# A scheduler's rules in a decay-attention and max-MoE kernel: VectorE and GpSimd kept apart, a price for matmuls that waited, new seeds

## The chip, the cores and the metric

The kernel runs on one core of one Trainium2 chip. The metric is the device time of one execution in microseconds (us), the median of several runs. The engines are TensorE (PE in the rows; its weight loads are PEld), VectorE (DVE), ScalarE (ACT), GpSimd (POOL) and SyncE (SP), which issues the DMAs.

## What is computed

Decayed causal attention over 8 batches of 8 heads, 576 positions, 64 columns a head; then a feed-forward block whose hidden layer is the largest of three products, over all 4608 tokens.

```python
scores = scale * np.matmul(q, k.transpose(0, 1, 3, 2))
cum = np.cumsum(np.log(np.clip(f, 0.0001, 1.0)), axis=-1)
scores = np.where(causal, -1e9, scores + cum[..., :, None] - cum[..., None, :])
attn = softmax(scores)
x = np.matmul(attn, v)            # then heads side by side: (4608, 512)
h = np.maximum(np.maximum(x @ w1, x @ w2), x @ w3)      # 512 -> 768
out = h @ w_out                                          # 768 -> 512
```

## The kernel before

The work is cut into 64 heads and 8 batches. A head's scores are built in two units of queries (256 and 320 wide) in PSUM banks `s`: a first pass of matmuls (`pass_a`, L730), the causal mask (on TensorE for the first 16 heads, on VectorE at L767 and L772 for the others), the column maxima on VectorE (`most`, L793 to L798), a GpSimd all-reduce over the partitions (L808) and, behind the first batch, a GpSimd copy of the result into a row of the query operand (L811), then a second pass that subtracts the maximum (L730 again, or L757 in the first batch) and the exponential on ScalarE (L829). From head 16 the sums of the exponentials are added on VectorE (L838 to L845) and all-reduced on GpSimd (L853); a row of them goes through DMA into a small tile `sc`, where VectorE adds a constant and inverts it (L1021, L1022). `values_pair` multiplies with v (L899).

A batch's feed-forward block follows when its heads are done. `gemm1` (L1059) runs 12 matmuls into one of four banks (`mp0`, `mp1`, `mp2`, `t`) for each of the three weights; ScalarE copies the first bank into `tm` (L1068), VectorE takes the maximum of the other two with `tm` (L1070), and each of these steps gives its bank back. Then a high and a low part are split off (L1073 on ScalarE, L1075 on VectorE) for `gemm2` (L1090). Heads of later batches are prepared meanwhile: VectorE transposes q and k (L619) and splits them (L625).

At the start, 20 matmuls on an identity (`warm_up`, L520) are there as filling; the first eight heads come in raw and TensorE turns them, six matmuls for each half (`turn_head`, L540), into the same four banks, which VectorE and ScalarE copy out (L548, L550). `decay` clips f on VectorE (L491), takes the logarithm on ScalarE (L493), the running sum on VectorE (L496), and ScalarE writes two rows of it (L500). Constants are set by memsets on GpSimd (L447, L461 to L473) and VectorE (L476).

The order of all this is not written out. Each step is added to a `Plan` with its engine, a cost in ns, its operands and a priority. `emit` walks through the steps like a clockwork: at the earliest moment an engine is free, it gives it the ready step with the best rank, books its cost (scaled and padded by `ROOM`), and lets a model of TensorE's clock and a lag for each pair of engines decide when others become ready. The instructions are then issued in the order of the booked beginnings; on the chip each engine follows its own list, and semaphores do the waiting. `SEEDS` disturb the ranks a little, one random stream for each window of priorities; a zero leaves a window alone.

Of the kernel before, what the change touches and what calls it, by code (L numbers as in the profile page):

```python
# [11 lines left out]
F32 = mybir.dt.float32  # L12
# [4 lines left out]
ALU = mybir.AluOpType  # L17
# [38 lines left out]
class Plan:  # L56
# [10 lines left out]
    ROOM = {"PE": (1.0, 0), "ACT": (1.0, -20.0), "DVE": (1.0, 0.0), "POOL": (1.0, 400.0), "SP": (1.0, 0)}  # L67
# [4 lines left out]
    SEEDS = [9961, 6458, 701, 7690, 5056, 2474, 4633, 0, 366, 8932, 0, 0, 1279, 0, 0, 723, 0, 0, 419]  # L72
# [10 lines left out]
    def add(self, eng, cost, fn, r=(), w=(), prio=0.0, xfer=0.0, rows=128, short=0.0, light=False, take=(), drop=()):  # L83
# [16 lines left out]
        self.steps.append((eng, cost, fn, deps, prio, xfer, rows, short, light, take, drop))  # L100

    def emit(self):
# [27 lines left out]
        short = 0.0  # L130
        clock = GatedClock()
# [19 lines left out]
        while done < n:  # L151
# [27 lines left out]
            if self.steps[i][5]:  # L179

                t = max(t, lanes[-8])
            begin[i] = t
# [53 lines left out]
def kernel(  # L236
# [212 lines left out]
    def head_constants(i, prio):  # L449

        for key, ns, go in (
            (f"ks{i}", 380, lambda: nc.gpsimd.memset(KS(i)[:, :, S:SP].bitcast(F32), 0.0)),
            (f"qs{i}", 1100, lambda: nc.gpsimd.memset(QS(i)[96:P, :, :].bitcast(F32), 1.0)),
            (f"ks{i}", 1100, lambda: nc.gpsimd.memset(KS(i)[96:P, :, 0:S].bitcast(F32), 0.0)),
            (f"ks{i}", 660, lambda: nc.gpsimd.memset(KS(i)[96:97, 1, :].bitcast(F32), -1.0)),
        ):
            add("POOL", ns, go, w=[key], prio=prio)
# [12 lines left out]
    add("POOL", 1060, sums_constants, ["cs"], [f"rs{g}{u}" for g in range(2) for u in (1, 2)], 0.0)  # L470
    add("POOL", 1100, constants, w=["const"], prio=-9)
    add("POOL", 200, lambda: nc.gpsimd.memset(LESS.bitcast(F32), 0.0), w=["less"], prio=-9)
    add("POOL", 100, lambda: nc.gpsimd.memset(LESS[0:1].bitcast(F32), -1.0), w=["less"], prio=-9)  # L473
    for i in range(H):
        add("POOL", 525, lambda i=i: first_constants(i), w=[f"qf{i}/2"], prio=-9 + i)
        add("DVE", 605, lambda i=i: nc.vector.memset(KF[i][64:P, :], 0.0), w=[f"kf{i}/2"], prio=-5.5 + 0.1 * i)  # L476
    add("POOL", 1650, value_constants, w=[f"vn{i}" for i in range(4)], prio=-8)


    def decay():  # L480
# [11 lines left out]
            ["pf1"], ["pf1"], DP)  # L492
# [5 lines left out]
            ["pf1"], ["pf1"], DP)  # L498
        for n in range(2):
# [4 lines left out]
            ["pf1"], [f"u{KT - 1}"], DP)  # L504
        for n, e, dst in [(n, n + 1, KF[n][64:65, :]) for n in (2, 3)] + [
# [4 lines left out]
            ["pf1"], ["cs"], DP)  # L510
        add("DVE", 669, lambda: nc.vector.scalar_tensor_tensor(
            cs[:, 1, :], ft, -1.0, cs[:, 0, :].bitcast(F32), op0=ALU.mult, op1=ALU.subtract),
            ["pf1", "cs"], ["cs"], DP)
# [40 lines left out]
    def convert(x, low, top, kt, kl, kx, prio):  # L554
# [5 lines left out]
            y, low, 29, None, op0=ALU.logical_shift_right), [kt], [kl], prio)  # L560
        add("DVE", 1.1 * n + 75, lambda: nc.vector.scalar_tensor_tensor(
            x, top, 3, y, op0=ALU.logical_shift_left, op1=ALU.bitwise_or), [kt, kl], [kx], prio)

    def split(x, h, l, kx, kh, kl, gone, prio):
# [3 lines left out]
            l(), x.bitcast(F32), h().bitcast(F32), op=ALU.subtract), kx + [kh], [kl], prio)  # L568
# [41 lines left out]
    def load_quad(b, g, prio):  # L610
        for nm, src, sc in (("q", q, scale), ("k", k, 1.0)):
# [9 lines left out]
            if b < NB32:  # L621
# [5 lines left out]
                op0=ALU.mult, op1=ALU.subtract), [key + "0"], [key + "1"], prio)  # L627
# [73 lines left out]
    def scores(n, unit, prio):  # L701
# [101 lines left out]
        for a, w, bk, col, nb in d["first"]:  # L803
# [5 lines left out]
            gm, mt, P, bass.bass_isa.ReduceOp.max), [km, km + "a"], [kg], prio - CB)  # L809
        if not first:  # L810
            add("POOL", 130 + 0.9 * nq, lambda: nc.gpsimd.tensor_copy(  # L811
                QS(s)[96:97, 1, q0:q0 + nq], gm[96:97, :]), [kg], [kx], prio - CB)
# [34 lines left out]
        if unit == 2:  # L847
            add("ACT", act_cost(P), lambda: nc.scalar.activation(
                blocks_sum()[:, 0:P], px()[:, 0:P], AF.Copy), [pk], ["s2/0"], prio + SP_)
            add("DVE", dve_cost(P), add_blocks, [pk], ["s2/1"], prio + SP_)  # L850
        else:
            add("DVE", sum(dve_cost(w) + 125 for w in (320, 320, 192, 64)) - 125, add_blocks, [pk], ["s1"], prio + SP_)
        add("POOL", 520 + 5.1 * nq, lambda: nc.gpsimd.partition_all_reduce(  # L853
            Z[:, q0:q0 + nq], blocks_sum()[:, q0:q0 + nq], P, bass.bass_isa.ReduceOp.add), [f"s{unit}"], [f"z{unit}"], prio + SP_)
# [119 lines left out]
    def finish_rows(g, prio):  # L974
# [13 lines left out]
        for t in range(2):  # L988
# [3 lines left out]
            for j in range(2):  # L992
# [3 lines left out]
                U(pi)[:, q0:S], U(pi)[:, q0:S], r, op=ALU.mult), [key, ku], [ku], prio)  # L996

    def split_first(kt, unit, prio):
# [3 lines left out]
        else:  # L1002
# [3 lines left out]
            l(), U(kt)[:, cs], h().bitcast(F32), op=ALU.subtract), [ku, kh], [kl], prio)  # L1006
# [6 lines left out]
    def finish_pair(pi, prio):  # L1013
# [18 lines left out]
        add("DVE", dve_cost(S), lambda: nc.vector.tensor_tensor(U(i), U(i), R(), op=ALU.mult), [f"u{i}", "r"], [f"u{i}"], prio)  # L1032

    def split_x(b, prio):
        for kt in range(KT):
# [4 lines left out]
                xl(kt), U(i), xh(kt).bitcast(F32), op=ALU.subtract), [f"u{i}", f"xh{kt}"], [f"xl{kt}"], prio)  # L1040
# [6 lines left out]
    def gemm1(b, c0, cn, fb, parts, prio):  # L1047
# [24 lines left out]
        for hh, hl, kh, kl, a, d, w in parts:  # L1072
# [4 lines left out]
                [kt_, kh + str(fb)], [kl + str(fb)], prio)  # L1077
# [171 lines left out]
```

## Time and profile before

| what | us |
|---|---|
| median of 3 runs | 909.21 |
| lowest and highest | 906.84, 911.02 |
| the profiled execution | 907.82 |
| its span, first to last instruction | 906.0 |
| TensorE busy in the span | 886.8 (98%) |
| VectorE busy | 634.5 (70%) |
| GpSimd busy | 429.0 (47%) |
| ScalarE busy | 382.0 (42%) |

Busy time of TensorE is read with care: a matmul's end is modelled, and a matmul that follows closely on another overlaps it. So a wait of TensorE is read from the idle time in front of a matmul and from the distance of the starts after it.

### The profile page before, as it was taken

The page shows a single profiled execution, that of the slowest core. Times are in us where ns is not written, and L with a number is a line of the kernel's source. Part 1 is how long each engine was busy: PE and PEld are TensorE (multiplying, and loading weights), DVE is VectorE, ACT ScalarE, POOL GpSimd, SP SyncE. Part 2 cuts the span into 40 slices and gives each one's busy share as a digit, 9 for nine tenths or more (in the row PEclk, how much of TensorE's full clock was granted, in tenths as well). Part 3 has the DMA queues.
Part 4 walks back from the last instruction along what each step waited for, and adds up shares of the span by engine and source line. Part 5 has one row for each costly group of instructions (what it writes and reads, how often), then busy time and mean ns, then how long its engine had stood idle before and what let it go on. Part 6 is the DMA issues. An engine that isn't in the chain of part 4 may idle for free.

```text
span 906.0 us, 18239 instructions
## 1 busy us (share of the span) xinstructions
PE 886.8 (98%) x6614; PEld 806.4 (89%) x6614; DVE 634.5 (70%) x1386; ACT 382.0 (42%) x882; POOL 429.0 (47%) x380
## 2 busy tenths in 40 slices
PE   7999999999999999999999999999999999999998
PEld 5888988889988998899989898988989898998997
DVE  6899764577878786887878786777867867662211
ACT  4797543444433443444433443343334443441211
POOL 4564132327574657456564556455454555740000
PEclk8999999999999999999999999999999999999999
DMA  6965256455564355455454544544444554301010
GB/s 159 327 198 178 80 140 158 119 132 145 123 176 118 97 149 124 128 131 140 108 158 127 120 129 118 139 106 130 114 108 133 117 145 121 93 14 37 1 36 24
DMA packets 93371, 110.99 MB, mean 123 GB/s; under 512 B 52461, under 2 KB 56301, under 8 KB 93282
## 3 DMA queue, kind: packets, MB, share of 16 engines
q1 hardware_dynamic: 93282, 109.83, 46.1%
q8 instruction: 53, 0.87, 0.4%
q14 instruction: 36, 0.29, 0.1%
HBM read 50.22 MB, written 9.87 MB: 66 GB/s over the span
## 4 chain that ended last, share of the span: by engine, by line
PE 80%; DVE 13%; issue 2%; ACT 2%; DMA 2%; SPq 1%; POOL 1%; ACTq 0%; DVEq 0%
PE mp L1059 31%; PE mp L1090 12%; PE s L730 11%; PE t L1059 10%; PE mp L899 6%; PE t L1090 3%; PE t L899 3%; DVE hl L619 2%; DVE va_s L845 2%; DVE mx L798 2%; DVE tm L1070 1%; PE t L866 1%; DVE hl L625 1%; DMA vn<-in_v_dram 1%; DVE hml_r L1075 1%
## 5 line engine op out<-in xcount | busy, mean ns | idle before, releaser
L1059 PE MATMUL mp<-xh_r,w_r 128*128 128x320 f32 (+1 forms) x1624 | 379.9, 299 | 2.3 <-DVE tm L1070 1.9
L1059 PEld LDWEIGHTS mp<-xh_r,w_r 128*128 128x128 f32 x1624 | 278.0, 188 | 6.4 <-DVE tm L1070 3.1
L808 POOL PARTITION_ALL_REDUCE gm<-mx x131 | 158.0, 1207 | 234.8 <-DVE mx L798 98.4
L853 POOL PARTITION_ALL_REDUCE z<-va_s x96 | 194.9, 2031 | 128.0 <-DVE va_s L845 54.4
L1059 PE MATMUL mp<-xl_r,w_r 128*128 128x320 f32 (+1 forms) x812 | 240.2, 296 | 0.0
L1059 PEld LDWEIGHTS mp<-xl_r,w_r 128*128 128x128 f32 x812 | 152.9, 188 | 0.7
L1059 PE MATMUL t<-xh_r,w_r 128*128 128x320 f32 (+1 forms) x536 | 143.5, 299 | 1.0 <-DVE tm L1070 1.0
L730 PEld LDWEIGHTS s<-qs_r,ks_r 128*128 128x128 f32 (+1 forms) x784 | 115.7, 181 | 17.4 <-issue 9.3
L730 PE MATMUL s<-qs_r,ks_r 128*128 128x320 f32 (+4 forms) x784 | 128.3, 281 | 1.5 <-issue 0.8
L798 DVE TENSOR_TENSOR mx<-mx,s 128x320 f32<-128x320 f32 (+3 forms) x248 | 92.1, 371 | 21.5 <-ACT mx L805 7.7
L1059 PEld LDWEIGHTS t<-xh_r,w_r 128*128 128x128 f32 x536 | 97.8, 188 | 2.7 <-DVE tm L1070 2.3
L1090 PE MATMUL mp<-w_r,hmh_r 128*128 128x512 f32 (+1 forms) x324 | 100.0, 391 | 0.0
L1070 DVE TENSOR_TENSOR tm<-mp,tm 128x320 f32<-128x320 f32 (+1 forms) x143 | 64.6, 452 | 48.3 <-PE mp L1059 33.3
L1073 ACT ACTIVATE hmh_r<-tm 128x256 fp32r<-128x256 f32 x96 | 40.0, 417 | 101.9 <-DVE tm L1070 101.6
L1059 PE MATMUL t<-xl_r,w_r 128*128 128x320 f32 (+1 forms) x268 | 79.3, 296 | 0.0
L619 DVE STREAM_TRANSPOSE hl<-hl 128x576 f32<-128x576 f32 x56 | 67.8, 1244 | 3.5 <-DMA vn<-in_v_dram 3.1
L1068 ACT ACTIVATE tm<-mp 128x256 f32<-128x256 f32 (+1 forms) x76 | 31.0, 408 | 85.8 <-PE mp L1059 80.4
L1090 PEld LDWEIGHTS mp<-w_r,hmh_r 128*128 128x128 f32 x324 | 57.2, 188 | 10.1 <-issue 0.7
L1075 DVE TENSOR_TENSOR hml_r<-tm,hmh_r 128x256 fp32r<-128x256 f32 x96 | 48.6, 506 | 20.3 <-ACT hmh_r L1073 20.2
L1090 PE MATMUL mp<-w_r,hml_r 128*128 128x512 f32 (+1 forms) x162 | 62.5, 386 | 0.0
L829 ACT ACTIVATE pf<-s 128x512 f32<-128x512 f32 (+4 forms) x107 | 49.5, 506 | 27.8 <-PE s L730 24.2
L767 DVE TENSOR_TENSOR s<-s,mask 128x256 f32<-128x256 f32 x96 | 40.6, 424 | 27.8 <-PE s L730 27.4
(253 smaller groups left out, 1485.9 us busy)
## 6 DMA issues: line engine op xcount, KB each, us to landing
qs_r<-hl SPq DMA_DIRECT2D x168, 144.0 KB
ks_r<-hl SPq DMA_DIRECT2D x168, 144.0 KB
w<-in_moe_w_dram SPq DMA_DIRECT2D x9, 1024.0 KB
out_dram<-o_r SPq DMA_DIRECT2D x35, 256.0 KB
hl<-in_k_dram SPq DMA_DIRECT2D x14, 576.0 KB
hl<-in_q_dram SPq DMA_DIRECT2D x14, 576.0 KB
r_r<-rdram SPq DMA_DIRECT2D x56, 144.0 KB
vn<-in_v_dram SPq DMA_DIRECT2D x30, 128.0 KB
```

The source lines that it names most:

```text
L619: add("DVE", 1085, lambda e=e, tt=tt, xs=xs: nc.vector.transpose(tt[:, e], xs[:, e]), [key + "0"], [key + "1"], prio)
L730: nc.tensor.matmul(bank[bk][0:l.shape[-1], col:col + w], l, rhs(qa, w), start=start and bk not in begun, stop=stop, skip_group_check=True)
L767: nc.vector.tensor_tensor(x, x, mask.rearrange("p (o x) -> p o x", o=1).broadcast_to((P, 2, P)), op=ALU.add)
L798: nc.vector.tensor_tensor(mt[:, a:a + w], mt[:, a:a + w], bank[bk][:, col:col + w], op=ALU.max)
L808: add("POOL", 450 + 2.6 * nq, lambda: nc.gpsimd.partition_all_reduce(gm, mt, P, bass.bass_isa.ReduceOp.max), [km, km + "a"], [kg], prio - CB)
L829: add("ACT", act_cost(w), lambda bk=bk, w=w, col=col: nc.scalar.activation(px()[:, col:col + w], bank[bk][:, 0:w], AF.Exp, scale=sc), [kb[ ...
L853: add("POOL", 520 + 5.1 * nq, lambda: nc.gpsimd.partition_all_reduce(Z[:, q0:q0 + nq], blocks_sum()[:, q0:q0 + nq], P, bass.bass_isa.Reduc ...
L899: nc.tensor.matmul(t[D * j:D * j + D, qa:qa + w], vn[:, j, c, 0:D], prs[x][j][0]()[:, col:col + w], start=y == 0, stop=True, skip_group_ch ...
L1059: nc.tensor.matmul(m(), unit_w(i, fb)[:, w, kt, :], xx, start=kt == 0 and x == 0, stop=kt == KT - 1 and x == 2,)
L1070: add("DVE", dve_cost(cn), lambda m=m: nc.vector.tensor_tensor(t, m(), t, op=ALU.max), [km, kt_], [kt_], prio + EV, drop=(slot,))
L1075: add("DVE", dve_cost(w), lambda hh=hh, hl=hl, a=a, d=d, w=w: nc.vector.tensor_tensor(hl()[:, fb, d:d + w], t[:, a:a + w], hh()[:, fb, d:d ...
L1090: nc.tensor.matmul(BANKS[slot.bank][:, 0:cn], l[:, fb, cs], unit_o(fb)[:, r, ds], start=fb == 0 and x == 0, stop=fb == FT - 1 and x == 2,)
```

## The change

No instruction of the computation is added or taken away. What changes is the planner's bookkeeping, and with it the order.

- A step may carry a `port` time. Two-operand steps of VectorE, and the `tensor_scalar` steps that go from SBUF to SBUF, carry 1 ns, which stands for their whole length: while such a step is booked, no GpSimd step with a port begins. A GpSimd step carries the part in which it holds VectorE's marked steps off: all of a memset, `2.1 * nq - 30` ns of a maximum's all-reduce, `4.45 * nq - 180` of a sum's, `0.6 * nq + 70` of a copy.
- GpSimd's padding in `ROOM` goes from 400 ns a step to 130 ns.
- A matmul that begins over 20 ns after TensorE became free is booked with 105 ns more (`STALL`).
- The seeds are new; 16 of 19 windows are now disturbed, where it was 12.

```diff
-    ROOM = {"PE": (1.0, 0), "ACT": (1.0, -20.0), "DVE": (1.0, 0.0), "POOL": (1.0, 400.0), "SP": (1.0, 0)}
+    ROOM = {"PE": (1.0, 0), "ACT": (1.0, -20.0), "DVE": (1.0, 0.0), "POOL": (1.0, 130.0), "SP": (1.0, 0)}
...
+    STALL = 105.0
...
+            port = self.steps[i][11]
+            if port:
+
+                t = max(t, held[e])
             begin[i] = t
...
             end = t + cost
+            if port:
+                other = "POOL" if e == "DVE" else "DVE"
+                held[other] = max(held[other], t + port if e == "POOL" else end)
             if e == "PE":
-                end = clock.run(t, cost, self.steps[i][6])
+                end = clock.run(t, cost + (self.STALL if t > free[e] + 20 else 0.0), self.steps[i][6])
...
         add("POOL", 450 + 2.6 * nq, lambda: nc.gpsimd.partition_all_reduce(
-            gm, mt, P, bass.bass_isa.ReduceOp.max), [km, km + "a"], [kg], prio - CB)
+            gm, mt, P, bass.bass_isa.ReduceOp.max), [km, km + "a"], [kg], prio - CB, port=2.1 * nq - 30)
```

Ten lines are added to the file, so a line behind L491 stands ten lower in the code after: L520 is L530, L1070 is L1080. The orders were compared with buffer numbers and semaphores. `DVE_49` and the like name the engine (or DMA queue) whose semaphore is waited for.

The first place is TensorE at the start, from the last transposition of head 1 to those of head 3 (`w8` holds heads 0 and 1, `w9` heads 2 and 3). Before:

```order
L540 MATMUL mp2_120<-hdl_107,w8_103 64x96 x5
L520 LDWEIGHTS ident_63
L520 MATMUL s10_113<-ident_63 128x512
...
L540 MATMUL mp0_118<-hdl_107,w9_104 64x96 [waits DMAHW7_49,Activation_49]
L540 MATMUL mp0_118<-hdl_107,w9_104 64x96 x5
L540 MATMUL mp1_119<-hdl_107,w9_104 64x96 [waits DMAHW6_49,Activation_49]
```

Now:

```order
L550 MATMUL mp2_120<-hdl_107,w8_103 64x96 x5
L530 LDWEIGHTS ident_63
L530 MATMUL s10_113<-ident_63 128x512
...
L550 MATMUL mp0_118<-hdl_107,w9_104 64x96 [waits DMAHW7_49,DVE_49]
L550 MATMUL mp0_118<-hdl_107,w9_104 64x96 x5
L530 LDWEIGHTS ident_63
L530 MATMUL s10_113<-ident_63 128x512
...
L550 MATMUL mp1_119<-hdl_107,w9_104 64x96 [waits DMAHW6_49,Activation_49]
```

Before, seven fillers stand ahead of the transposition into `mp0`; now two stand ahead of it and five behind. The copies that empty `mp0` have changed places too: the transposition waited for ScalarE's copy as the second, and now for VectorE's.

The second place is VectorE and GpSimd at the start. VectorE before:

```order
L522 CAST hdl_107<-ident_63 128x128 [waits Pool_49]
L476 MEMSET ks1_68 64x576
L476 MEMSET xh_69 64x576 x2
L476 MEMSET xl_70 64x576
L491 TENSOR_SCALAR pf1_80<-pf1_80 65x576 [waits DMAHW1_49,DMAHW0_49]
...
L496 SCALAR_TENSOR_TENSOR pf1_80<-pf1_80 65x576 [waits Activation_49]
L548 COPY qs0_65<-mp0_118 64x288 [waits PE_49]
```

and now:

```order
L532 CAST hdl_107<-ident_63 128x128 [waits Pool_49]
L486 MEMSET ks1_68 64x576
L486 MEMSET xh_69 64x576 x2
L501 TENSOR_SCALAR pf1_80<-pf1_80 65x576 [waits DMAHW1_49,DMAHW0_49]
L486 MEMSET xl_70 64x576 x2
L506 SCALAR_TENSOR_TENSOR pf1_80<-pf1_80 65x576 [waits Activation_49]
L558 COPY qs0_65<-mp0_118 64x288 [waits Activation_49]
```

(between L491 and L496 before stood the second memset of `xl`). One memset moved from ahead of the clipping of f to behind it. GpSimd before:

```order
L447 MEMSET qs0_65 64x576 [waits Pool_49]
L472 MEMSET pl2_72 128x128 [waits Pool_49]
L461 MEMSET vn0_75 64x2x65 [waits Pool_49]
...
L473 MEMSET pl2_72 1x128
L447 MEMSET qs1_66 64x576 [waits Pool_49]
L447 MEMSET ks0_67 64x576
```

and now:

```order
L482 MEMSET pl2_72 128x128
L457 MEMSET qs0_65 64x576 [waits Pool_49]
L483 MEMSET pl2_72 1x128
L457 MEMSET qs1_66 64x576
L471 MEMSET vn0_75 64x2x65
...
L457 MEMSET ks0_67 64x576 [waits Pool_49]
```

The eight short memsets of the v buffers moved behind `qs1`, and four memsets in a row (`qs0` to `vn0`) now begin without a wait between them.

The third place is VectorE in the middle of the kernel, around the eleventh step of L1021. Before:

```order
L767 TENSOR_TENSOR s10_113<-s10_113,mask_64 128x2x128
L1021 TENSOR_SCALAR sc_94<-sc_94 64x18
L772 TENSOR_TENSOR s11_114<-s11_114,mask_64 128x64
L619 STREAM_TRANSPOSE hl_73<-hl_73 128x18x32
L1022 RECIPROCAL sc_94<-sc_94 64x18
L1070 TENSOR_TENSOR tm1_112<-mp2_120,tm1_112 128x320
```

and now:

```order
L777 TENSOR_TENSOR s2_116<-s2_116,mask_64 128x2x128
L1031 TENSOR_SCALAR sc_94<-sc_94 64x18
L803 COPY mx2_83<-s2_116 128x128
L805 TENSOR_REDUCE mx2_83<-s2_116 128x128
L1032 RECIPROCAL sc_94<-sc_94 64x18
L852 TENSOR_TENSOR va1_s_2091<-pf1_80 128x320
```

The next maximum that gives a bank back stood four steps behind L1021; now 16 steps lie between.

## Rows read from the trace of the kernel before

**Rows 1.** Busy time by stretch (PE, PEld, DVE, ACT, POOL; clock; DMA).

```profile
24.00:91.00 67.00, 62.95 (x512) 57.84 (x512) 61.24 (x104) 55.04 (x110) 35.79 (x32) 1.00 0.75 230
91.00:861.00 770.00, 763.64 (x5615) 694.86 (x5614) 551.22 (x1240) 308.13 (x731) 382.66 (x319) 1.00 0.46 117
```

**Rows 2.** TensorE's waits: us in total, times, longest; those for banks.

```profile
PE mp L1059 <- DVE tm L1070: 1.9, 4, 1.1
PE t L1059 <- DVE tm L1070: 1.0, 3, 0.7
...
PE mp L899 <- DVE tm L1070: 0.6, 1, 0.6
PE mp L899 <- ACT tm L1068: 0.6, 1, 0.6
...
PE t L899 <- DVE tm L1070: 0.4, 1, 0.4
PE mp L1059 <- ACT tm L1068: 0.3, 1, 0.3
```

**Rows 3.** Timeline, one wait of TensorE: start, us, engine, line; [idle before].

```profile
376.04 0.31 PE L1059 MATMUL mp<-xh_r,w_r 128*128 128x320 f32 x1
377.45 0.42 PE L1059 MATMUL mp<-xh_r,w_r 128*128 128x320 f32 x1 [1.10 <-DVE tm L1070]
377.70 0.31 PE L1059 MATMUL mp<-xl_r,w_r 128*128 128x320 f32 x1
377.85 0.45 PE L1059 MATMUL mp<-xh_r,w_r 128*128 128x320 f32 x2
```

**Rows 4.** Timeline of VectorE and GpSimd ahead of that wait.

```profile
374.34 1.37 DVE L1021 TENSOR_SCALAR sc<-sc 64x18 f32<-64x18 f32 x1
...
372.35 4.11 POOL L853 PARTITION_ALL_REDUCE z<-va_s  x2 [0.84 <-DMA sc<-z]
```

**Rows 5.** Shortest, median and longest of one line's steps on VectorE, ns.

```profile
L1021 DVE TENSOR_SCALAR sc<-sc x28: 139/160/1366, 133.6 to 813.3; 64x18 f32<-64x18 f32 x28
L1075 DVE TENSOR_TENSOR hml_r<-tm,hmh_r x96: 386/424/1502, 97.7 to 895.9; 128x256 fp32r<-128x256 f32 x96
L798 DVE TENSOR_TENSOR mx<-mx,s x248: 186/355/491, 20.0 to 799.3; 128x320 f32<-128x320 f32 x56, 128x192 f32<-128x192 f32 x56, 128x160 f32<-128x160 f32 x4, 128x32 f32<-128x32 f32 x4
```

**Rows 6.** Timeline of the start, VectorE.

```profile
2.82 0.23 DVE L522 CAST hdl<-ident 128x128 f32<-128x128 bf16 x1
...
5.04 0.54 DVE L476 MEMSET xl<- 64x576 f32 x1
5.61 3.21 DVE L491 TENSOR_SCALAR pf<-pf 65x576 f32<-65x576 f32 x1
...
10.85 0.43 DVE L548 COPY qs<-mp 64x288 f32<-64x288 f32 x1
```

**Rows 7.** Timeline of the start, GpSimd.

```profile
2.67 0.20 POOL L472 MEMSET pl<- 128x128 f32 x1
...
4.82 0.57 POOL L447 MEMSET qs<- 64x576 f32 x1
...
7.42 1.09 POOL L447 MEMSET xl<- 64x576 f32 x2
8.57 1.26 POOL L465 MEMSET ph<- 97x1152 f32 x1
```

**Rows 8.** Timeline of the start, ScalarE's first copy and TensorE.

```profile
11.07 0.41 ACT L550 ACTIVATE qs<-mp 64x288 f32<-64x288 f32 x1
...
13.34 1.83 PE L540 MATMUL mp<-hdl,w 96*64 96x96 f32 x24 [3.75 <-ACT qs L550]
```

**Rows 9.** Busy time by stretch around the clock's fall, columns as in the first.

```profile
10.34:13.76 3.42, 0.42 (x10) 0.42 (x12) 1.66 (x4) 3.33 (x8) 0.00 (x0) 1.00 0.33 76
13.76:20.58 6.82, 6.82 (x58) 6.51 (x55) 2.45 (x7) 3.28 (x9) 0.00 (x0) 0.50 0.54 130
```

**Rows 10.** Timeline of GpSimd, a maximum's all-reduce over 256 columns.

```profile
369.98 1.06 POOL L808 PARTITION_ALL_REDUCE gm<-mx  x1 [1.77 <-DVE mx L795]
```

More of the change, by code (lines that the diff above doesn't have):

```diff
@@ L81, in lend, with add @@
         self.owed.append(set(self.read.get(key, ())) | ({self.wrote[key]} if key in self.wrote else set()))
-    def add(self, eng, cost, fn, r=(), w=(), prio=0.0, xfer=0.0, rows=128, short=0.0, light=False, take=(), drop=()):
+    def add(self, eng, cost, fn, r=(), w=(), prio=0.0, xfer=0.0, rows=128, short=0.0, light=False, take=(), drop=(),
+            port=0.0):
         i = len(self.steps)
@@ L99, in add @@
         deps.discard(i)
-        self.steps.append((eng, cost, fn, deps, prio, xfer, rows, short, light, take, drop))
+        self.steps.append((eng, cost, fn, deps, prio, xfer, rows, short, light, take, drop, port))
     def emit(self):
@@ L130, in emit @@
         short = 0.0
+        held = {"DVE": 0.0, "POOL": 0.0}
         clock = GatedClock()
@@ L456, in head_constants @@
         ):
-            add("POOL", ns, go, w=[key], prio=prio)
+            add("POOL", ns, go, w=[key], prio=prio, port=ns)
     def value_constants():
@@ L468 @@
     nc.gpsimd.load_library(next(x for x in all_libraries if any(c.__name__ == "InstPartitionAllReduce" for c in x.instructions)))
[L470 to L473, printed above, removed]
+    add("POOL", 1060, sums_constants, ["cs"], [f"rs{g}{u}" for g in range(2) for u in (1, 2)], 0.0, port=1060.0)
+    add("POOL", 1100, constants, w=["const"], prio=-9, port=1100.0)
+    add("POOL", 200, lambda: nc.gpsimd.memset(LESS.bitcast(F32), 0.0), w=["less"], prio=-9, port=200.0)
+    add("POOL", 100, lambda: nc.gpsimd.memset(LESS[0:1].bitcast(F32), -1.0), w=["less"], prio=-9, port=100.0)
     for i in range(H):
-        add("POOL", 525, lambda i=i: first_constants(i), w=[f"qf{i}/2"], prio=-9 + i)
+        add("POOL", 525, lambda i=i: first_constants(i), w=[f"qf{i}/2"], prio=-9 + i, port=525.0)
         add("DVE", 605, lambda i=i: nc.vector.memset(KF[i][64:P, :], 0.0), w=[f"kf{i}/2"], prio=-5.5 + 0.1 * i)
-    add("POOL", 1650, value_constants, w=[f"vn{i}" for i in range(4)], prio=-8)
+    add("POOL", 1650, value_constants, w=[f"vn{i}" for i in range(4)], prio=-8, port=1650.0)
     def decay():
@@ L497, in decay @@
             fx, lx, lx, 0.0, op0=ALU.add, op1=ALU.bypass),
-            ["pf1"], ["pf1"], DP)
+            ["pf1"], ["pf1"], DP, port=1.0)
         for n in range(2):
@@ L559, in convert @@
         add("DVE", 0.72 * n + 40 if y is low else 0.85 * n, lambda: nc.vector.tensor_scalar(
-            y, low, 29, None, op0=ALU.logical_shift_right), [kt], [kl], prio)
+            y, low, 29, None, op0=ALU.logical_shift_right), [kt], [kl], prio, port=1.0)
         add("DVE", 1.1 * n + 75, lambda: nc.vector.scalar_tensor_tensor(
-            x, top, 3, y, op0=ALU.logical_shift_left, op1=ALU.bitwise_or), [kt, kl], [kx], prio)
+            x, top, 3, y, op0=ALU.logical_shift_left, op1=ALU.bitwise_or), [kt, kl], [kx], prio, port=1.0)
     def split(x, h, l, kx, kh, kl, gone, prio):
@@ L626, in load_quad @@
                 hl[:, 1], hl[:, 1].bitcast(F32), sc, hl[:, 0].bitcast(F32),
-                op0=ALU.mult, op1=ALU.subtract), [key + "0"], [key + "1"], prio)
+                op0=ALU.mult, op1=ALU.subtract), [key + "0"], [key + "1"], prio, port=1.0)
     def vbuf(pi):
```

30 lines of the change are left out of this document (15 added, 15 removed).

## The prediction

> **What bounds the kernel now.** I read the busy time by stretch first. From 91 to 861 us TensorE is busy for 763.64 of 770 us [rows 1]; nothing else comes near, so only what lies between its matmuls can be won there. Its instructions are the same before and after. I also counted in the two orders the places where a score matmul of 64 or 128 columns stands ahead of a full weight load, which it is too short to hide: 191 before and 189 now. So the work itself is no term of the sum; the terms are waits.
>
> Next the table of waits. Behind the start, most of TensorE's idle time with a named cause is a wait for a bank which VectorE's L1070 or ScalarE's L1068 has still to give back: 11 waits, 4.8 us of idle time [rows 2]. One wait costs more than its idle time. In the timeline of the longest [rows 3], starts are 0.15 us apart when nothing waits (377.70 to 377.85). Across the wait they are 1.41 us apart, 1.26 too much against the 1.10 shown, and the next distance is 0.25 instead of 0.15. So each wait costs about 0.16 + 0.10 = 0.26 us beyond its idle time, and the 11 cost 4.8 + 11 x 0.26 = 7.7 us.
>
> Then why the banks come late. Ahead of that wait VectorE's L1021 took 1.37 us [rows 4], where its median is 0.16 [rows 5]; a GpSimd all-reduce of sums ran across it. The same shows line by line: L1075, with both operands in SBUF, goes from 0.39 to 1.50 us, while L798, which reads one operand from PSUM, never goes over 0.49 [rows 5]. So a two-operand or SBUF-to-SBUF step of VectorE can be held by a GpSimd step for up to 1.2 us, and the planner of before knows nothing of it: it counts on a bank that comes up to 1.2 us later.
>
> Last the start. There TensorE stands idle for 3.75 us until 13.34, and after this stretch, with 0.42 us of work in 3.42, the granted clock falls to 0.50, which is 1.2 instead of 2.4 GHz, for 6.82 us of unbroken work [rows 8, 9].
>
> **The change part by part.** *Port times and the stall's price* (taken together, since both act through the order). They remove no hold on the chip: the same steps collide as often, and nothing makes GpSimd wait. What they do is book the hold, so that TensorE's list places the next use of a bank where the bank is really free, and fills in score matmuls until then. At the third place shown of the order that can be seen: the step that was held by 1.2 us no longer has a bank's release four steps behind it. The bounds are 0 (every wait avoided comes back elsewhere) and -7.7 us (all 11 waits gone, rows 2 and 3). I take half, -3.8: the bookings of port times are lengths by formula, the real hold depends on which of the two engines is first, and an order this tight makes some new collisions.
>
> *GpSimd's padding, 400 to 130 ns.* Behind an all-reduce and its copy the second score pass is now booked 2 x 0.27 = 0.54 us sooner. No row of TensorE's waits behind the start names GpSimd, so the old padding was enough. The new booking for 256 columns is 450 + 666 + 130 = 1246 ns, against 1.06 us in the timeline [rows 10]. It still covers them, so I take 0. If that cover is gone, a second pass waits for up to 0.54 us, plus the 0.26 of any wait.
>
> *The start.* In the first place of the order the transposition into `mp0` now waits for VectorE's copy. That copy waits for ScalarE's first one, which ends at 11.48 [rows 8]; with some 0.15 for the hand-over (an estimate; in rows 6 VectorE starts 0.03 us behind its own last step, and a semaphore comes on top) and 0.43 for the copy [rows 6], `mp0` is free at about 12.1, not 13.3. But what follows, `mp1`, still needs ScalarE's copies behind L500, which need the scan. The scan now has one more memset ahead of it, 0.54 us [rows 6], and so the next banks come at about the old times. The last of the four transpositions ends some 0.7 us sooner at half clock, 1.2 at full.
>
> The five fillers now stand inside the stretch that was empty. With them and one transposition it holds about 1.7 us of work instead of 0.42. Whether that keeps the clock up no row can show, so I bound it: nothing, or half of what remains at low clock, from 16.3 to 20.58, 2.1 us. The start is thus worth -0.7 to -3.3 us. From 24 to 91 us VectorE is busy for 61.24 of 67 us [rows 1], and some of a head start will be lost there to its queue. I take the upper end, as the stretch is no longer empty, and two thirds of it: -2.0.
>
> In this I take it that the clipping of f (L491) is not helped. It took 3.21 us and ended at 8.82, just when GpSimd's row of memsets made its first pause, from 8.51 to 8.57 [rows 6, 7]. Now it stands one memset (0.54 us) sooner. Its predecessor L522 began at 2.82 and took 0.23, with a memset beside it until 2.87 [rows 6, 7], so that row does not tell whether it can be held as well. In the new order four memsets run there without a pause, until about 3.64 (an estimate from the lengths of 0.20 and 0.57 in rows 7). If L522 is held like L491, which is also one SBUF input and an SBUF output, VectorE comes 0.8 us late to the pauses between the short memsets, the last of which ends at about 5.2 by the same lengths, and L491 sits behind the long ones again. I take that, as L491 is the nearest row.
>
> The Trainium skill, SBUF — State Buffer, section "Who interferes with whom", says that a cast, like `tensor_scalar`, can use both of VectorE's port pairs and then blocks fully against any GpSimd step; by that rule L522 is held, the sum stays at 903.4, and without it the rival below would hold.
>
> *Sum.* The profiled execution took 907.82 us, with 1.82 outside its span of 906.0. 907.8 - 3.8 + 0 - 2.0 = 902.0. The median of the runs of before is 1.4 above the profiled execution, so the forecast for the median is **903.4 us**.
>
> **The rivals.** *Waits only change places* (0.23). Every filler that TensorE puts into one wait is missing at another, and VectorE's total stays at 551 of 770 us [rows 1]. For it: nothing physical is removed. Against it: the held steps were the largest error of the old bookings. Then the 11 waits come back in other places, the start gives 0.7, and the median is 909.2 - 0.7 = 908.5.
>
> *The cast is not held* (0.15). Then L491 stands at 5.0 before a pause of GpSimd's at about 5.1 to 5.2, and ends near 5.4 rather than 8.8. Logarithm, scan and the first copies come up to 3.4 us sooner, the wait of 3.75 us shrinks to what the DMAs leave, and the clock has no reason to fall. The start then gives about 5 instead of 2.0: 903.4 - 3 = 900.4. For it: L522's row, 0.23 us beside a memset. Against it: L491's own.
>
> *GpSimd's smaller padding makes new waits* (0.12), the one that ends slower. Its place is the second score pass of the 56 later heads, two units each, 112 in all. If a GpSimd step is held by VectorE longer than booked, TensorE waits for it at a mean of half of 0.54, with 0.26 on top: 0.53 us. From about 20 of the 112 on this outweighs the gain and gives a time over 913.8; with 22 it is 903.4 + 11.7 = 915. Against it: a length in rows 10 below the new booking, and no wait of this kind before.
>
> **How the numbers follow.** The forecast's case has 0.50, the others as given. The likeliest case gives 903.4, by itself from 898 (both terms at their full size, -3.3 and -7.7, with 1.4 added back) to 907 (half a term). A tenth of the cast rival lies below 897, the padding rival and a few of the moved waits above 911; that leaves out under 2 in 10, so the range is 897 to 911. A change of 0.5%, 4.5 us, is about what a measurement of this kernel can tell from none; the limits are 904.7 and 913.8. Two thirds of the forecast's case lie below 904.7 (0.33), all of the cast rival (0.15) and a little of the moved waits (0.03): 0.51 faster. The padding rival and a trace of the others make 0.12 slower. The rest, 0.37, is within the limits.
>
> **What would show it.** In the profile after, TensorE's waits for L1080 and L1078 (the lines L1070 and L1068 of before) should be five or six, near 2 us of idle time; if there are again 11, the port times did nothing. The longest steps of L1085 and L1031 should still reach over 1.2 us, since nothing removes the hold. A row that names GpSimd as what TensorE waited for behind 91 us would speak for the padding rival. At the start, L501 should end near 8.8 (5.4 if the cast is not held), the transposition into `mp0` should begin near 12.1, and the granted clock from 13.76 to 20.58 should be 1.00. If the clock falls again, the start is worth 0.7 at most; if waits for DMAs grow in the middle, a queue that I left aside has moved.

## The result and the profile after

| | before | after |
|---|---|---|
| median (runs) | 910.11 us (5; 906.84 to 911.02) | 896.31 us (5; 894.38 to 897.49) |
| ratio, 95% interval | | 0.9854 (0.9832 to 0.9877) |
| profiled execution, its span | 907.82, 906.0 | 896.01, 893.8 |

The change is worth 13.8 us, where 5.8 were forecast: right in sign, and 0.7 us below the range. A second set of four runs gave 896.29 (e16, below). Line numbers are ten higher after than before.

Busy time by stretch, with the columns of [rows 1], which these two rows answer:

```profile
24.00:91.00 67.00, 64.83 (x518) 60.36 (x519) 59.70 (x104) 56.51 (x115) 37.98 (x32) 1.00 0.72 217
91.00:861.00 770.00, 766.58 (x5620) 699.09 (x5620) 544.56 (x1231) 304.44 (x723) 378.44 (x317) 1.00 0.46 118
```

TensorE, in the first column behind the stretch's length, is busy for 766.58 of 770 us instead of 763.64. The whole table of its waits, which answers [rows 2], is short now:

```profile
PE s L740 <- DMA ks_r<-hl: 2.9, 2, 2.5
PE s L530 <- POOL ident masks.py:199: 1.5, 1, 1.5
PE t L876 <- ACT pf L839: 1.2, 2, 0.8
PE s L740 <- ACT pf L839: 0.6, 2, 0.4
PE mp L550 <- DVE qs L558: 0.5, 1, 0.5
PE s L740 <- DMA sc<-z: 0.4, 1, 0.4
PE mp L876 <- ACT ph L890: 0.3, 1, 0.3
```

No wait for a bank from L1080 or L1078 (L1070 and L1068 before) is left in it; a single one of 0.05 us stands in the timeline. What has grown is its first row, waits for loads of keys: a single one of 0.4 us stood there before.

To see where the time went, I summed TensorE's instructions, each at the usual distance to its successor in the trace of before, and read how much earlier the changed kernel reaches the same sum. This lead is 5.7 us at about 34 us of its time, 7.9 at 106, only 3.0 at 132, and 11.8 at the end; the two profiled executions differ by 11.8. So there are four parts: the start (+5.7), the stretch to 106 us (+2.2), a loss of 4.9 us around 117 us, and the middle (+8.8). By TensorE's gaps of over 30 ns the last part is 5.9 us less idle time (6.36 to 0.47 us); the other 2.9 lie in the same instructions standing closer together (761.0 to 758.0 us in all). Of these 2.9, the 15 waits that are gone account for 4.0, at 0.26 to 0.28 us each beyond their idle time (how this is read stands in the part on why the prediction was wrong); the other distances between starts grew by 1.1.

The start on VectorE (start, length, us), to set beside [rows 6]:

```profile
2.82 0.27 DVE L532 CAST hdl<-ident 128x128 f32<-128x128 bf16 x1
...
5.05 0.46 DVE L501 TENSOR_SCALAR pf<-pf 65x576 f32<-65x576 f32 x1
```

The clip of f took 0.46 us and not 3.21. GpSimd gave way this time, in its last short memset (0.12 us usually), before its long row ([rows 7]), so it is not true that nothing makes GpSimd wait:

```profile
4.88 0.20 POOL L471 MEMSET va<- 64x130 f32 x1
5.14 0.42 POOL L472 MEMSET va<- 128x10 f32 x1
5.62 1.09 POOL L457 MEMSET ks<- 64x576 f32 x2
```

TensorE's wait of 3.75 us [rows 8] became one of 0.50 us for `mp0`, in brackets here, and behind it the engine runs on:

```profile
8.71 0.72 PE L550 MATMUL mp<-hdl,w 96*64 96x96 f32 x12 [0.50 <-DVE qs L558]
...
12.45 0.71 PE L740 MATMUL s<-qs 128*128 128x160 f32 x4
```

The granted clock, 0.50 from 13.76 to 20.58 before [rows 9], is 1.00 there. At 117 us it is the other way round. The timeline first, then the busy time by stretch (clock in the third column from the end):

```profile
114.59 0.30 PE L931 MATMUL mp<-ph_f,rx_r 128*32 128x160 f32 x1
117.43 0.41 PE L740 MATMUL s<-qs_r,ks_r 128*128 128x256 f32 x2 [2.54 <-DMA ks_r<-hl]
```

```profile
114.00:117.43 3.43, 0.89 (x22) 0.57 (x14) 2.77 (x6) 1.41 (x6) 1.06 (x1) 1.00 0.85 215
117.43:118.93 1.50, 1.50 (x13) 1.50 (x14) 1.06 (x4) 0.54 (x1) 0.69 (x3) 1.00 0.96 349
118.93:122.34 3.41, 3.41 (x18) 3.41 (x17) 2.21 (x3) 2.16 (x6) 1.45 (x2) 0.50 0.83 252
```

TensorE stood for 2.54 us, and 1.5 us later its clock fell to half for 3.41 us, at a cost of 1.7 (half of it, all of it being busy). With a wait of 0.41 us for the same kind of load at 108.57 that is 4.7 of the 4.9 us.

Holds were not removed. The longest L1085 (L1075 before) is still 1447 ns; the longest L1031 (L1021) is 944 instead of 1366, where the prediction's sign was over 1.2 us for both (shortest, median, longest, as in [rows 5]):

```profile
L1031 DVE TENSOR_SCALAR sc<-sc x28: 138/169/944, 127.5 to 801.5; 64x18 f32<-64x18 f32 x28
L1085 DVE TENSOR_TENSOR hml_r<-tm,hmh_r x96: 352/423/1447, 89.8 to 884.1; 128x256 fp32r<-128x256 f32 x96
```

### The profile page after: what moved, and what is told of

The parts are those of the page before. It is cut to its first block, busy times and chain, and to the rows that moved or that the text cites. A ratio compares the mean times of both kernels' runs of the same rounds, so it can differ in the third digit from the quotient of the medians.

```text
span 893.8 us, 18201 instructions
## 1 busy us (share of the span) xinstructions
PE 883.0 (99%) x6614; PEld 804.7 (90%) x6614; DVE 627.8 (70%) x1386; ACT 381.0 (43%) x882; POOL 428.9 (48%) x380
## 4 chain that ended last, share of the span: by engine, by line
PE 93%; SPq 2%; ACT 2%; DVE 1%; DMA 1%; issue 1%; DVEq 0%; ACTq 0%
PE mp L1069 38%; PE t L1069 13%; PE s L740 12%; PE mp L1100 12%; PE mp L909 7%; PE t L1100 5%; PE t L909 2%; PE t L876 2%; SPq L660 1%; DMA ks_r<-hl 1%; SPq L982 1%; PE mp L931 1%; PE s L767 1%; PE mp L740 0%; PE mp L550 0%
## 5 line engine op out<-in xcount | busy, mean ns | idle before, releaser
L1069 PE MATMUL mp<-xh_r,w_r 128*128 128x320 f32 (+1 forms) x1616 | 370.8, 299 | 0.0
L1069 PEld LDWEIGHTS mp<-xh_r,w_r 128*128 128x128 f32 x1616 | 274.3, 188 | 3.2 <-issue 1.5
L1069 PE MATMUL t<-xh_r,w_r 128*128 128x320 f32 (+1 forms) x544 | 140.8, 299 | 0.0
L740 PEld LDWEIGHTS s<-qs_r,ks_r 128*128 128x128 f32 (+1 forms) x784 | 116.5, 181 | 16.7 <-issue 9.6
L1080 DVE TENSOR_TENSOR tm<-mp,tm 128x320 f32<-128x320 f32 (+1 forms) x148 | 66.9, 452 | 65.8 <-PE mp L1069 50.8
L1100 PE MATMUL mp<-w_r,hmh_r 128*128 128x512 f32 (+1 forms) x300 | 93.3, 393 | 0.0
L777 DVE TENSOR_TENSOR s<-s,mask 128x256 f32<-128x256 f32 x96 | 40.9, 428 | 29.2 <-PE s L740 28.8
L1100 PEld LDWEIGHTS mp<-w_r,hmh_r 128*128 128x128 f32 x300 | 51.8, 188 | 10.1 <-issue 2.7
L821 POOL CAST qs_r<-gm 1x256 fp32r<-1x256 f32 (+1 forms) x112 | 55.0, 491 | 7.2
L1100 PE MATMUL mp<-w_r,hml_r 128*128 128x512 f32 (+1 forms) x150 | 57.8, 385 | 0.0
L1078 ACT ACTIVATE tm<-mp 128x256 f32<-128x256 f32 (+1 forms) x67 | 27.7, 413 | 70.0 <-PE mp L1069 69.7
```

The lines of the kernel that those rows point to most:

```text
L740: nc.tensor.matmul(bank[bk][0:l.shape[-1], col:col + w], l, rhs(qa, w), start=start and bk not in begun, stop=stop, skip_group_check=True)
L777: nc.vector.tensor_tensor(x, x, mask.rearrange("p (o x) -> p o x", o=1).broadcast_to((P, 2, P)), op=ALU.add)
L821: add("POOL", 130 + 0.9 * nq, lambda: nc.gpsimd.tensor_copy(QS(s)[96:97, 1, q0:q0 + nq], gm[96:97, :]), [kg], [kx], prio - CB, port=0.6 * ...
L1069: nc.tensor.matmul(m(), unit_w(i, fb)[:, w, kt, :], xx, start=kt == 0 and x == 0, stop=kt == KT - 1 and x == 2,)
L1080: add("DVE", dve_cost(cn), lambda m=m: nc.vector.tensor_tensor(t, m(), t, op=ALU.max), [km, kt_], [kt_], prio + EV, drop=(slot,))
L1100: nc.tensor.matmul(BANKS[slot.bank][:, 0:cn], l[:, fb, cs], unit_o(fb)[:, r, ds], start=fb == 0 and x == 0, stop=fb == FT - 1 and x == 2,)
```

## The experiments

Where steps are moved by hand, the plan is made as ever and only its emitted order is changed:

```diff
-        for i in sorted(range(n), key=lambda j: (begin[j], j)):
+        for i in moved_row(self, sorted(range(n), key=lambda j: (begin[j], j)), ...):
```

### The start

**e1**: the changed kernel with the clip L501 one memset later on VectorE, as before.

> The kernel after, with one edit: VectorE's clipping of f (L501) stands behind one more memset, as in the kernel before; all other lists are those of after. Theory that the start's gain comes from the clipping being let in at a pause between GpSimd's short memsets: it now comes 0.6 us later, meets the long memsets, takes over 3 us and ends near 9.1; TensorE's first wait grows to some 3 us, and the time rises from 896.3 by 5 to 8 us, to 901 to 904. Rival, that the start's gain comes from where the fillers and transpositions stand on TensorE: the clipping costs its 0.6 us at most, 896.3 to 897.

896.05 us (4 runs; ratio 0.9861, 0.9829 to 0.9893): the rival's time, though its cause is not shown by it, since the clip was not held here either. It asked at 5.66 and took 0.54 us. It was let in between two of GpSimd's long memsets, the pair of which took 1.40 us instead of 1.09.

**e2**: the kernel before with the clip L491 one memset earlier, nothing else.

> The kernel before, with VectorE's clipping of f (L491) one memset earlier and nothing else. Theory of the pause: at 5.04 GpSimd's row of long memsets has begun in this order, so the clipping still ends near 8.8 and the time is that of before, 910 within 1. Rival, that the clipping's place alone is what counts: it ends near 5.5 and the time falls to 903 to 905.

902.36 us (7 runs; 0.9935, 0.9914 to 0.9955). My account by pauses is wrong; one moved step of VectorE brings the start, with the seven fillers on TensorE where they were. TensorE's wait fell from 3.75 to 1.04 us, no low clock is left until 899 us, and the lead is 6.2 us at 129 us and 5.9 at the end:

```profile
10.30 1.21 PE L540 MATMUL mp<-hdl,w 96*64 96x96 f32 x24 [1.04 <-ACT qs L550]
```

**e3**: e2 with GpSimd's memsets of the v buffers moved behind `qs1` too.

> The kernel before, with the clipping one memset earlier and GpSimd's eight short memsets of the v buffers behind the second long one, as in after; TensorE's, ScalarE's and SyncE's lists are those of before, seven fillers ahead of the transposition included. Theory of the pause: the clipping takes about 0.5 us and ends near 5.5, TensorE's wait of 3.75 us falls below 1 us, the granted clock from 13.76 to 20.58 is 1.00, and the time falls by 5 to 7 us, to 903 to 905. Rival, that the fillers' place on TensorE is what kept the clock up: the clock still falls and the time is 907 to 910.

902.04 us (5 runs; 0.993, 0.990 to 0.996), no more than e2.

**e5**: the kernel before once more, one execution, for its profile.

> The kernel before once more, unchanged, for one more profile. If the clip of the gate row (VectorE, line 491, 3.21 us from 5.61 to 8.82) was held by GpSimd's memsets as a matter of their order, it is held here too, 3 us and more, with its end between 8.5 and 9. If its length was an accident of that one execution (the four clips at 5.00 to 5.66 of the other kernels took 0.46 to 0.70 us), it takes 0.5 to 1.1 us here, the first transposition into mp0 comes 3 us earlier and the span is 3 us under the 906.0 of the first profile. The waits of TensorE on VectorE behind 91 us stand either way, nine to eleven of them.

The hold is no accident: 3.22 us again, and the span is 906.7.

```profile
5.61 3.22 DVE L491 TENSOR_SCALAR pf<-pf 65x576 f32<-65x576 f32 x1
```

With the runs below, nineteen traces show one regularity. Where the clip asked beside the first memset of a row that GpSimd runs without a pause, it got in behind that memset (e2, e11, e12, e14: asked at 5.00 to 5.01, the row began at 4.82, 0.70 us; e1: asked at 5.66, the row began at 5.32, 0.54 us) or still among the short ones (after, e3, e4, e6, e8, e9, e10 and e15 to e17: 0.46 to 0.56 us). Where it asked beside the second (before, e5, e7, e13: asked at 5.61, the row from 4.82), it was held until the row's end, 3.21 to 3.22 us. These four have the same steps in the same order there, so the hold is one case seen four times. Either half of the changed order, VectorE's (e2) or GpSimd's (e1), is enough to avoid it. Why the second memset differs from the first no run tells.

### The wait at 117 us

**e4**: the changed kernel with the first of two loads of the last half of `w_out` (L612, issued at 106.43 us in the midst of the heads' loads) and the ScalarE step that reads it moved behind those loads.

> The kernel after, with the first half of the last w_out load (L612, and the ScalarE step that reads it) moved behind the second pair of heads' loads; nothing else moves. Theory: this load of half a megabyte between the heads' loads makes ks_r land late, which is TensorE's wait of 2.54 us at 117 and of 0.41 at 108 and the fall of the clock behind it, 4.9 us in all. Without it 3 to 5 us go: 891.5 to 893.5. Rival, that the heads' loads are late by their own issues and small packets: the wait at 117 stays over 1.5 us, 895 to 897.

897.03 us (4 runs; 0.9871, 0.9838 to 0.9905); the lead at 132 us stays at 2.7. The scores that had waited for keys began 1.25 us sooner, and the next in line took the keys' place: a score bank of ScalarE's, then GpSimd's copy L821. The clock fell here too, to 0.50 from 118.61 to 122.03 us.

```profile
116.18 0.44 PE L740 MATMUL s<-qs_r,ks_r 128*128 128x256 f32 x2 [1.17 <-ACT pf L839]
...
118.90 0.64 PE L740 MATMUL s<-qs_r,ks_r 128*128 128x320 f32 x1 [1.40 <-POOL qs_r L821]
```

**e15**: seven steps of gemm 1 (21 matmuls) put on TensorE ahead of the scores that wait.

> The changed kernel with seven steps of gemm 1 put in front of the scores that wait for the key load at 117.43 us. If the 4.9 us lost there are a wait without work (2.54 us), a matmul that waited (0.26) and the clock at half speed behind it (3.41 us, 1.7 lost), 4 to 5 us come back: 891 to 893, with the clock at 1.00 there. If the heads' steps themselves are late (the key load, then GpSimd's copy at line 821), the wait only comes behind the seven steps, shorter by their 2.5 us but there again for other scores: 893 to 896.

894.86 us (4 runs; 0.9855, 0.9837 to 0.9873), the second case. Part of the wait came back behind the seven steps, now for a bank; the clock did not fall (1.00 from 5.4 us to the end of the matmuls), and the lead at 132 us is 5.9 instead of 3.0. Some of that is only work done earlier: at 160 us it is 4.8 instead of 2.9, and 13.5 instead of 11.8 at the end.

```profile
116.80 0.28 PE L1069 MATMUL mp<-pl_xa,w_r 128*128 128x256 f32 x1
116.92 0.34 PE L740 MATMUL s<-qs_r,ks_r 128*128 128x256 f32 x2
117.11 0.29 PE L756 MATMUL s<-mask,ident 128*128 128x128 bf16 x2
117.21 0.89 PE L740 MATMUL s<-qs_r,ks_r 128*128 128x320 f32 x5
119.56 0.67 PE L740 MATMUL s<-qs_r,ks_r 128*128 128x320 f32 x4 [1.47 <-ACT pf L839]
```

**e16, e17**: the changed kernel and e15 again, on one chip.

> The changed kernel once more, unchanged, beside the next one on the same chip: 896.3 again (895 to 897.5), with the wait of 2.5 us for the key load at 117.4 us and the clock at half speed for 3.4 us behind it.

> The changed kernel with seven steps of gemm 1 ahead of the scores that wait at 117 us, once more, beside the changed kernel on the same chip. If the 2.9 us that its lead kept there in the profile are real, it is 1.5 to 3 us faster than its neighbour, 893.5 to 895. If they are lost again in the middle, within 1 us of it.

896.29 us (4 runs; 0.9857, 0.9837 to 0.9877) and 893.93 us (5 runs; 0.9839, 0.9817 to 0.9862). The filled one has the lower median by 2.4 us, the lowest of all versions here, though single runs overlap (893.09 to 897.16 against 894.06 to 897.20), and so do the intervals: the medians alone do not prove it. The granted clock tells more. Of the nine executions of the filled order (e15, e17), seven kept a mean of 1.000 and took 893.09 to 895.09 us, and the two that did not took 897.16; of the nine of the changed kernel (the result's and e16's), one did, at 894.06. The stretch in which the changed kernel had its low clock, first in e16 and then in e17:

```profile
117.84:121.25 3.41, 3.41 (x18) 3.41 (x17) 2.95 (x5) 2.01 (x4) 1.48 (x2) 0.50 0.94 281
```

```profile
117.84:121.25 3.41, 2.60 (x22) 2.18 (x21) 2.83 (x5) 2.97 (x8) 1.48 (x2) 1.00 0.89 285
```

At half clock e16 is busy throughout and issues 18 matmuls; e17 rests for 0.81 us and issues 22.

### Rules and seeds, one at a time

Each is an edit in one place, and each gives another order throughout.

```diff
-            if port:
-
-                t = max(t, held[e])
```

**e8** (above: no booking of the ports).

> The changed kernel without the port's rule alone (the charge for a matmul that waited, the pad of 130 and the new seeds stay). If the port's booking removed the waits in the middle, they come back, eight or more with 3 to 5 us together, the lead grows by less than 3 us behind 135 us, and the time is 901 to 908. If the charge for a matmul that waited is what removed them (it makes the planner avoid any wait of TensorE), they stay away: under 1.5 us together, and the time is 894 to 899.

**e9** (`STALL = 0.0`).

> The changed kernel without the charge of 105 for a matmul that waited, all else as it is, the new seeds too. If the charge is what keeps TensorE's waits away in the middle, eight or more waits on the evictions stand behind 91 us, 3 to 6 us together, and the time is 902 to 910. If it only rounds the plan's times, the order stays close to that of the changed kernel and the time is 895 to 899. If nineteen seeds fit one set of rules alone (as the runs with one half of the change say so far: 912.4, 912.3 and 908.6), the time is 904 to 913 with waits of all kinds, at the start too.

**e10** (GpSimd's pad at 400).

> The changed kernel with the old pad of 400 on GpSimd's steps, all else as it is, the new seeds too. If the pad is worth nothing by itself (the prediction took it at 0) and the order hangs on the rest, the time is 895 to 900. If the smaller pad brings gain in the middle, the waits of TensorE behind 91 us are 3 to 5 us more than the changed kernel's 0.5 and the time is 900 to 904. If the seeds fit one set of rules alone, it is 904 to 913.

**e6** (the rules of before with the new `SEEDS`) and **e7** (the new rules with the old ones).

> The kernel before with the nineteen seeds of the changed one and none of its rules. If the rules do the work in the middle (VectorE's and GpSimd's shared time is booked), the waits of TensorE on the evictions' steps stay, eight or more of them behind 91 us with 4 to 5 us together, and the time is 903 to 911. If the seeds are what found the better order, the waits are gone here too and the time is 896 to 900.

> The changed kernel with the seeds of the one before. If the rules do the work, the waits of TensorE on VectorE behind 91 us are under 1.5 us together and the lead over the kernel before grows by 7 to 9 us from 135 us to the end, as with the new seeds; the time is 894 to 900. If the seeds do it, eight or more such waits stand, the lead grows by less than 3 us and the time is 902 to 908.

**e11, e12** (`SEEDS = [0] * 19`, under the new rules and under the old).

> The changed kernel with all nineteen seeds at 0: the rules with no search behind them. Beside it stands the kernel before with its seeds at 0. If the rules make better plans by themselves, this one is 4 us or more faster than that one and has fewer waits of TensorE on evictions behind 91 us. If the gain comes from the search of seeds under the rules, the two lie within 3 us of one another, at 908 to 918, and both have eight or more such waits.

> The kernel before with all nineteen seeds at 0, the other half of the pair: 912 to 920 if the new rules by themselves are worth 4 us or more, 908 to 918 and within 3 us of the other if not. Its clip of the gate row shows whether an order without a search has the 3 us hold at the start.

Measured, with TensorE's waits of over 30 ns behind 91 us in each profile (number and us; "bank" is those on the evictions L1070 and L1068, or the lines that answer to them), and the time at half clock in the whole execution, its very end with it:

| kernel | median us | ratio (interval) | bank waits | all waits | half clock us |
|---|---|---|---|---|---|
| port booked: after | 896.31 | 0.9854 (0.9832 to 0.9877) | 1, 0.05 | 4, 3.42 | 5.9 |
| e7, old seeds | 912.27 | 1.0038 (1.0020 to 1.0056) | 5, 3.56 | 11, 5.71 | 16.5 |
| e9, no stall | 912.74 | 1.0051 (1.0033 to 1.0068) | 6, 4.05 | 12, 11.21 | 19.7 |
| e10, pad 400 | 929.43 | 1.0223 (1.0199 to 1.0246) | 4, 2.67 | 14, 17.89 | 29.5 |
| e11, no seeds | 916.06 | 1.0083 (1.0061 to 1.0104) | 7, 2.03 | 15, 12.87 | 19.2 |
| not booked: before | 910.11 | | 12, 4.90 | 17, 6.36 | 10.2 |
| e6, new seeds | 912.35 | 1.0044 (1.0028 to 1.0060) | 12, 7.45 | 20, 11.03 | 8.5 |
| e8, all but port | 908.63 | 1.0008 (0.9989 to 1.0028) | 10, 3.88 | 16, 7.28 | 7.1 |
| e12, no seeds | 915.77 | 1.0084 (1.0056 to 1.0113) | 10, 5.40 | 17, 11.06 | 10.5 |

Two things follow. The port's booking does what it says: with it 1 to 7 bank waits, without it 10 to 12, whatever the seeds; their idle time is 2.5 us in the mean of five against 5.4 in the mean of four (single ones overlap: 4.05 in e9, 3.88 in e8). And that is not what sets the time. The rules without seeds are worth nothing (916.06 against 915.77), and every half of the change alone leaves the kernel where it was or slower. The other waits, for loads, for GpSimd's copies, for ScalarE, and the low clock behind the long ones, differ by far more from order to order. e10, 20 us behind before, has three of 2.6 to 4.6 us, all for the heads' scores (total, times, longest):

```profile
PE s L740 <- DMA out_dram<-o_r: 4.6, 1, 4.6
PE s L740 <- DMA qs_r<-hl: 3.9, 1, 3.9
...
PE s L740 <- DMA ks_r<-hl: 2.6, 1, 2.6
```

Of the nine orders in the table only that of the changed kernel is good in all respects at once. What the nineteen numbers and the rules add to each other can't be divided between them. Four of these times lie outside the cases stated for them: e6 and e8 just above (by 1.4 and 0.6 us), e7, which has less than half of the bank waits and yet took 912.27, and e10, 16 us above its slowest case. e10 can't tell the pad from the order that came with it, so what the pad is worth by itself stays open.

### Nine evictions by hand

In the kernel before, ten of the twelve bank waits end with a VectorE eviction (L1070), and VectorE had no idle time in front of any of the ten: they stood in its queue. The one of 376.98 us had ScalarE's and TensorE's part from 374.18 on, and stood behind five other steps of VectorE's. **e13** moves nine of them up by one to three places in VectorE's order; **e14** has these and the clip.

```diff
+    ('DVE', 1070, 14, 1), ('DVE', 1070, 30, 2), ('DVE', 1070, 62, 3),
+    ('DVE', 1070, 86, 1), ('DVE', 1070, 94, 1), ('DVE', 1070, 110, 1),
+    ('DVE', 1070, 112, 1), ('DVE', 1070, 148, 1), ('DVE', 1070, 154, 2),
```

(engine, line, which one, places)

> The kernel before with nothing changed but nine evictions of feature block 1 (VectorE, line 1070): each is put one to three steps earlier in VectorE's own order, in front of a step that is not in a hurry. They are those behind nine of TensorE's twelve waits on an eviction (159.87, 234.67, 377.45, 487.11, 513.87, 583.20, 589.51, 746.48 and 760.11 us; 3.9 us of idle time in the profile). If those waits are a matter of VectorE's order and are worth their idle time and 0.26 us each, this is 3.9 and 2.3, so 6.2 us faster, at 902 to 904.5, with the rest as it was. If a wait taken away only moves to the next one that is late, the time stays at 907 to 910.

> The same nine evictions and the clip of the gate row one memset earlier (the edit that gave 902.36 alone), and no rule of the change. If start and middle add up, 895 to 898, as fast as the changed kernel by ten moved steps. If they don't, 900 to 903.

e13: 906.86 us (12 runs; 0.9979, 0.9967 to 0.9991); e14: 901.03 us (6 runs; 0.9928, 0.9910 to 0.9947), 1.3 us below e2, with intervals that overlap. Start and middle add up (7.3 us, against e2's 6.2 and e13's 1.5), but the middle is small: in the medians a quarter of what I put down (1.5 of 6.2). In the profile of e13 all nine waits are gone, and 12 waits of 3.57 us are left of 17 of 6.36. New ones took some of it back. The largest follows some microseconds behind the place of the longest of the nine:

```profile
381.38 0.41 PE L1059 MATMUL mp<-xh_r,w_r 128*128 128x320 f32 x1 [0.83 <-ACT tm L1068]
```

Its eviction on ScalarE stood behind two steps that read VectorE's transpositions:

```profile
378.76 2.25 ACT L623 ACTIVATE hl<-hl 128x1152 fp32r<-128x1152 f32 x2 [0.60 <-DVE hl L619]
380.91 0.42 ACT L1068 ACTIVATE tm<-mp 128x320 f32<-128x320 f32 x1
```

The move did not bring this about. In the kernel before, the same two steps stand ahead of the same eviction:

```profile
380.56 2.25 ACT L623 ACTIVATE hl<-hl 128x1152 fp32r<-128x1152 f32 x2 [0.60 <-DVE hl L619]
382.71 0.41 ACT L1068 ACTIVATE tm<-mp 128x320 f32<-128x320 f32 x1
```

There TensorE, held up by its wait at 377.45, came to that bank at 383.48, when it was free. In e13 ScalarE's two steps come 1.8 us sooner than in the kernel before, while TensorE, without that wait, comes 3.1 us sooner. So it meets the next eviction that is late: its lead goes from 1.8 to 3.1 us at 375 us and is back at 2.0 behind the new wait.

From 135 us to the end its lead grows by 2.4 us, less than the 2.8 of idle time that went. The waits that went were worth their price of 0.27 us each on top, but other distances between starts grew by 1.6.

## Why the prediction was wrong

*The start: the step that failed.* The prediction put the start at -2.0, since it took the cast (L522, now L532) to be held behind four memsets and the clip therefore to come late. The cast was let in at once (0.27 us from 2.82), and the clip took 0.46. The four memsets did not run without a pause, as the prediction had it; short pauses like its own of 8.51 to 8.57 lie between them, at 2.76 and at 3.00:

```profile
2.19 0.57 POOL L457 MEMSET qs<- 64x576 f32 x1
2.81 0.19 POOL L483 MEMSET pl<- 1x128 f32 x1
3.04 0.57 POOL L457 MEMSET qs<- 64x576 f32 x1
```

Its rival "the cast is not held" had the mechanism, and 5.4 for the clip's end (5.51 measured), at a chance of 0.15; but with 5 us even it was small, for the start came to 5.7. Its sum by bounds, -0.7 to -3.3, was no bound, because it held the clip fixed. e2 shows what that place alone is worth: 6.2 us, in the profile's lead and in the medians. And the premise behind it, that a held step must wait for a pause of GpSimd's row, fell with e1 and e2: the clip entered between two long memsets. The Trainium skill, SBUF — State Buffer, section "Who interferes with whom", says that whichever of the two engines begins first has the ports for its whole instruction. One instruction is what e1 and e2 show; the rest of a row, with five more memsets, in before, e5, e7 and e13 is more than that rule gives.

*The stretch to 106 us* stood in the sum at nothing, or a loss; it gave 2.2 more. The waits of before at 42 to 74 us (0.55, 0.58, 0.81, 0.58 and 1.42 us the longest) became 0.34, 0.31, 0.36, 0.28 and 0.83.

*The middle: sized at half.* The mechanism held: the rule books the hold and does not remove it (L1085 as long as ever, as the prediction said), and bank waits fall by half wherever it stands, which is the half I took. But the order that was built has almost none left, and its other waits went as well: 8.8 us where 3.8 was the forecast and 7.7 the bound. The bound counted bank waits alone. The price of 0.26 us per wait beyond its idle time was right. It shows when each distance between two starts is set against the usual one (the median) of the same instruction in the trace of before: into a matmul that waited, the distance is 0.16 to 0.17 us longer than the idle time explains, and the four distances behind it are 0.10 to 0.13 longer together, so 0.26 to 0.29 a wait. This holds in each of the fifteen traces without a low clock between 135 and 890 us, with 2 to 17 waits each. From there on before has 17 waits, worth 4.5 us beyond their idle time, after 2, worth 0.6, and e13 12, worth 3.3. All other distances together are 28.1 us above the usual ones in before, 29.2 in after and 29.7 in e13, which hides part of the price; why they differ is open. So the 8.8 us are 5.9 of idle time and 4.0 of price, less 1.1; the bank waits alone are worth 7.8 of it, as the bound said, and the other waits 2.1, which the sum left out.

*The wait at 117 us* was not foreseen. The prediction's list of signs had it in one half-sentence (a queue left aside has moved), and that is what happened: the first of the two `w_out` loads (L612) stood at 106.43 amid the heads' loads, where before both (at 99.88 and 102.12) stood ahead of them. e4 shows that this one load is not the whole of it. The loss of 4.9 us, by itself nearly as large as the forecast's gain, hid a gain of 16.7.

*GpSimd's pad at 0*: no wait of TensorE behind 91 us names GpSimd, so that cover held; the worth of 0 itself no run shows (e10). The slow rival (0.12) did not come. *Waits only change places* (0.23) is wrong for the change but partly right for a change by hand (e13).

*The range* stopped at 897 because both terms were thought full at once only at 898. Had the cast's rival been put together with a full middle, 907.8 - 5 - 7.7 + 1.4 = 896.5, it would have reached the result.

## What to carry to other kernels

When a planner's rules or seeds change, read the new order itself at the two or three places where the engine that bounds the time stands longest; the order, and not what a rule is for, sets the time, and a single step moved (the clip, 6 us) can be worth more than all the rules together, which without seeds were worth nothing here. Take a rule's effect apart from the order it came with by counting the waits it aims at over several orders, since the medians of such orders differ by 33 us here for other reasons. And ask of each queue that the prediction leaves aside what its loads would do if they moved by 5 us, because waits of 2.4 to 2.9 us were each followed by 3.41 us of low clock here (after, e1, e16).

## What was not expected of the hardware

- A VectorE step that GpSimd's memsets can hold off (the clip) got in at the next boundary between memsets in fifteen traces and was held for 3.2 us, over five more of them, in four (before, e5, e7, e13); the two kinds differ in whether it asked beside the first or the second memset of an unpaused row.
- The wait of 2.54 us at 117 us was followed by 3.41 us at 0.50 of the clock, that of 2.93 us in e16 likewise, and in the nineteen traces each of the fifteen waits of 2.17 us or more has such a stretch beside it or behind it. Below that it went either way. Waits of 1.47 (e15), 0.81 and 1.39 us (e17) were not followed by one; one of 1.17 us in e4 was. At the start, 3.75 and 3.92 us of idle time (before, e13) brought 6.83 and 3.41 us of it. Nor is it plainly a matter of length: waits of 0.58 and 1.42 us a few us apart, between 64 and 74 us, stand in both profiles of the kernel before and in those of e2, e3, e13 and e14, and in e3 and e5 alone 3.41 us at 0.50 come with them.
- A matmul that waited cost TensorE 0.26 to 0.29 us beyond the idle time, in each of fifteen traces.
